# Fourier mixing with a SoLU layer on one core: the down products of a unit taken four steps behind its h instead of three

## The chip, the cores and the metric

The kernel runs on one core of a Trainium2 chip. The metric is the device time of one execution in microseconds, as the median of three runs. Before the change it is 1402.14 us (1400.0, 1402.14 and 1403.6).

## The reference, cut to what matters

Two blocks follow one another. The first is the real part of a Fourier transform over the sequence and the features of x, 8 x 3136 x 256. The second treats each of the 25088 rows of that result as a token.

```python
X = np.fft.fft(np.fft.fft(x, axis=1), axis=2).real      # 8 x 3136 x 256
h = X.reshape(25088, 256) @ w_in                        # 256 -> 1024
e = np.exp(h - h.max(-1, keepdims=True))
solu = h * e / (e.sum(-1, keepdims=True) + 1e-9)
ln = (solu - mean(solu)) / sqrt(var(solu) + 1e-6) * g_ln
out = ln @ w_out                                        # 1024 -> 256
```

## The kernel before

**Tiling.** The batch is worked on in four pairs of sequences. The sequence transform of 3136 = 49 x 64 points is split in two: a first transform over the 49 (transform1, L151), whose result goes through DRAM to be turned (the tile zd, written by SP at L156; the tile g, read by POOL at L163), and a second one over the 64 (transform2, L174 and L176). The feature transform is folded into the matrix Wi, so the product with Wi gives h at once. By symmetry only 25 of the 49 residues k1 are transformed; each gives two groups of 128 rows of the output, of signs 0 and 1 (k1 = 0 gives one).

A **unit** is one pair p and one k1. There are 100 units, and the main loop runs one step per unit. The steps in which a unit is worked on are these:

- `up` (L200): 8 matmuls of 128 x 512 on PE give the even and the odd part of h in PSUM, in the tiles ps_h.
- `even` (L206) and `join` (L214, L219) on DVE put the parts together into h for each sign, with its maximum. `expo` (L225) on ACT takes the exponential into u.
- `product` (L233) on DVE makes u = h * u, `square` (L242) on ACT and a few small POOL instructions (`stats`) give the variance and so the factor rs of each row.
- `turn_blocks` (L269): DVE transposes u in blocks of 32 x 32 into the tile v. `move_blocks` (L278): 16 DMAs on SP bring the blocks of two units to their places in the tile uT. Two following units share a batch, and a batch has one tile v and one tile uT; of each there are two buffers. A batch is moved once its second unit is through, at the end of every odd step. In the last two steps each unit is moved alone.
- `down` (L284): for each sign 8 products of 128 x 128 by 128 x 256 with Wo (16 matmuls in the trace) into a PSUM tile ps_o. `scale` (L289) on ACT multiplies by rs, and one step later `store` writes the rows, sign 0 with SP (L300) and sign 1 with an indirect DMA on POOL (L296).

**The order.** It is written out by hand: `tc.manual_schedule()` keeps each engine's instructions in the order of the program, and only waits on data and buffers move them. In a step i, PE runs: up of unit i, transform2 of unit i+1, one piece of transform1 for the next pair (or POOL turns a piece of g), then the down products of an older unit, i - lag. DVE runs even, join, product and the transposes of unit i, then the fold of the next pair's input (L111 to L113), if it is due. SP runs the store of unit i - lag - 1, then a write of zd, then the moves of the batch, then loads of x.

The first transform of the next pair is worked on in steps k1 = 4 to 19 of the first three pairs, 48 steps in all; its turn in the steps 20 to 24.

The lines that matter around the change:

```python
small = ctx.enter_context(tc.tile_pool(name="small", bufs=6))
...
lag = 3
for i in range(len(units) + lag):
    old = units[i - lag] if i >= lag else None
    if i > lag:
        store(units[i - lag - 1])
...
    if old:
        ps_o = [down(old, s) for s in old.signs]
```

The pool small holds the per-row statistics of a unit (rs among them), in as many buffers for each name as bufs says.

Of the kernel before, what the change touches and what calls it, by code (L numbers as in the profile page):

```python
# [33 lines left out]
def kernel(  # L34
# [33 lines left out]
    zpool = ctx.enter_context(tc.tile_pool(name="zpool", bufs=2))  # L68
    gpool = ctx.enter_context(tc.tile_pool(name="gpool", bufs=6))
    qpool = ctx.enter_context(tc.tile_pool(name="qpool", bufs=3))  # L70
    small = ctx.enter_context(tc.tile_pool(name="small", bufs=6))
    dram = ctx.enter_context(tc.tile_pool(name="dram", bufs=2, space=bass.MemoryType.DRAM))
    ps_h = ctx.enter_context(tc.tile_pool(name="ps_h", bufs=1, space=PSUM))
    ps_m = ctx.enter_context(tc.tile_pool(name="ps_m", bufs=4, space=PSUM))
# [91 lines left out]
    def transform2(pr, k1):  # L166

        i, k = divmod(k1, KG)  # L170
        g = pr.g[i]
        ps = ps_m.tile([P, KD * P + 1], FP32, tag="m", name="ps2")
        for h in range(KD):
            nc.tensor.matmul(ps[:, h * P : (h + 1) * P], g[:, k, h * P : (h + 1) * P], T[:, k1, :],  # L174
                             start=(h == 0), stop=True, skip_group_check=True)
        nc.tensor.matmul(ps[:, KD * P :], T[:, k1, :], g[:, k, P : P + 1],  # L176
                         start=False, stop=True, skip_group_check=True)
        return ps

    def take2(ps):  # L180
        q = qpool.tile([P, KD * P + 1], FP32, tag="q", name="q")
        nc.scalar.copy(q, ps)  # L182
        return q
# [11 lines left out]
    def up(t, c):  # L195

        ps = ps_h.tile([P, FF], FP32, tag=f"h{c}", name=f"ps_h{c}")
        for half in range(2):
            fs = slice(half * HW, (half + 1) * HW)
            nc.tensor.matmul(ps[:, fs], t.q[:, c * P : (c + 1) * P], Wi[:, c, fs], start=True, stop=True)  # L200
        return ps

    def even(t, ps):

        t.ev = fpool.tile([P, FF], FP32, tag="ev", name="ev", bufs=1)
        nc.vector.scalar_tensor_tensor(out=t.ev, in0=w_mid, scalar=t.q[:, KD * P :], in1=ps,  # L206
                                       op0=ALU.mult, op1=ALU.add)

    def join(t, ps):

        t.nmax = small.tile([P, 2], FP32, tag="nmax", name="nmax")
        for s in t.signs:
            t.h[s] = fpool.tile([P, FF], FP32, tag="h", name="h", bufs=2)
            nc.vector.tensor_tensor_reduce(out=t.h[s], in0=t.ev, in1=ps, scale=1.0, scalar=-3.0e38,  # L214
                                           op0=ALU.subtract if s else ALU.add, op1=ALU.max,
                                           accum_out=t.nmax[:, s : s + 1])
        n = len(t.signs)
        t.neg = small.tile([P, 2], FP32, tag="neg", name="neg")
        nc.vector.tensor_scalar(out=t.neg[:, 0:n], in0=t.nmax[:, 0:n], scalar1=-1.0, scalar2=None, op0=ALU.mult)  # L219

    def expo(t):
        t.esum = small.tile([P, 2], FP32, tag="esum", name="esum")
        for s in t.signs:
            t.u[s] = fpool.tile([P, FF], FP32, tag="u", name="u", bufs=2)
            nc.scalar.activation(out=t.u[s], in_=t.h[s], func=ACT.Exp, bias=t.neg[:, s : s + 1],  # L225
                                 accum_out=t.esum[:, s : s + 1])

    def product(t, s):

        if s == 0:  # L230
            t.usum = small.tile([P, 2], FP32, tag="usum", name="usum")
            t.nmean = small.tile([P, 2], FP32, tag="nmean", name="nmean")
        nc.vector.scalar_tensor_tensor(out=t.u[s], in0=t.h[s], scalar=1.0, in1=t.u[s], op0=ALU.mult,  # L233
                                       op1=ALU.mult, accum_out=t.usum[:, s : s + 1])
        nc.gpsimd.tensor_scalar(out=t.nmean[:, s : s + 1], in0=t.usum[:, s : s + 1], scalar1=-1.0 / FF,  # L235
                                scalar2=None, op0=ALU.mult)

    def square(t, s):

        if s == 0:  # L240
            t.ssq = small.tile([P, 2], FP32, tag="ssq", name="ssq")
        nc.scalar.activation(out=t.h[s], in_=t.u[s], func=ACT.Square, bias=t.nmean[:, s : s + 1],  # L242
                             accum_out=t.ssq[:, s : s + 1])
# [36 lines left out]
    def down(t, s):  # L280
        uT = t.batch.uT[:, t.w].rearrange("p c i (n s) -> p c (i n) s", s=2)
        ps = ps_m.tile([P, D], FP32, tag="m", name="ps_o")
        for c in range(KF):
            nc.tensor.matmul(ps, uT[:, c, :, s], Wo[:, c, :], start=(c == 0), stop=(c == KF - 1))  # L284
        return ps
# [5 lines left out]
    def store(t):  # L291

        for s in t.signs:
            if s:
                i = NP * NC + t.p * (NK - 1) + t.k1 - 1
                dma = nc.gpsimd.indirect_dma_start(  # L296
                    out=out, out_offset=bass.IndirectOffsetOnAxis(ap=idx[:, i : i + 1], axis=0),
                    in_=t.ot[s], in_offset=None)
            else:
                dma = nc.sync.dma_start(out=out_k[t.p, t.k1], in_=t.ot[s])  # L300

            tc.declare_no_dep(dma.ins, group=f"out{1 - s}", reason="other rows of the output")
            tc.add_to_no_dep_group(f"out{s}", dma.ins)
# [92 lines left out]
    def ahead(pr, step):  # L396

        c, r = divmod(step - 2, 2)
        if step == 0:
            load(pr, 0)  # L400
            load(pr, 1)
        elif 0 <= c < NC:
            if r == 0:
                add_mirror(pr, c)
            else:
                fold(pr, c)
                if c + 2 < NC:
                    load(pr, c + 2)

    def ahead_pe(pr, step):  # L410

        if 0 <= step - 4 < NH // 2:
            transform1(pr, step - 4)
        elif step - 4 >= NH // 2:
            turn(pr, step - 4 - NH // 2)

    with tc.manual_schedule():
        pairs = [Pair(p) for p in range(NP)]
        nc.sync.dma_start(out=idx, in_=mirror)
        nc.scalar.dma_start(out=F, in_=f_tab)  # L420
        ahead(pairs[0], 0)
        nc.vector.memset(ones, 1.0)
        nc.vector.memset(neg_half, -0.5)
        nc.vector.memset(T, 0.0)
        with tc.tile_pool(name="prep", bufs=1) as prep:
            prepare = load_weights(prep)
            for step in range(1, NK):
                ahead(pairs[0], step)
                ahead_pe(pairs[0], step)
            prepare()  # L430
        fpool = ctx.enter_context(tc.tile_pool(name="fpool", bufs=2))

        units = [Unit(p, k1) for p in range(NP) for k1 in range(NK)]
        units[0].q = take2(transform2(pairs[0], 0))
        lag = 3
        for i in range(len(units) + lag):
            cur = units[i] if i < len(units) else None
            nxt = units[i + 1] if i + 1 < len(units) else None
            old = units[i - lag] if i >= lag else None
            ahd = pairs[cur.p + 1] if cur and cur.p + 1 < NP else None  # L440
            last = i >= len(units) - 2
            if i > lag:
                store(units[i - lag - 1])
            if cur:
                if i % 2 == 0:
                    batch = Batch()
                cur.batch, cur.w = batch, i % 2
                even(cur, up(cur, 0))
                odd = up(cur, 1)
            if nxt:  # L450
                nxt.q = take2(transform2(pairs[nxt.p], nxt.k1))
            if cur:
                join(cur, odd)
                expo(cur)
            if ahd:
                ahead_pe(ahd, cur.k1)
            if old:
                ps_o = [down(old, s) for s in old.signs]
            if cur:
                for s in cur.signs:  # L460
                    product(cur, s)
                for s in cur.signs:
                    square(cur, s)
                    turn_blocks(cur, s)
            if old:
                scale(old, 0, ps_o[0])
            if cur:
                if last:
                    move_blocks(batch, slice(cur.w, cur.w + 1))
                elif cur.w:  # L470
                    move_blocks(batch, slice(0, 2))
                stats(cur)
            if ahd:
                ahead(ahd, cur.k1)
            if old and 1 in old.signs:
                scale(old, 1, ps_o[1])
        store(units[-1])
# [76 lines left out]
```

## Time and profile before

| | |
|---|---|
| median of three runs | 1402.14 us (1400.0 to 1403.6) |
| profiled execution | 1403.22 us, its span 1401.4 us |
| mean granted clock of TensorE | 0.935 of full speed |
| busy share | PE 87%, DVE 69%, ACT 44%, POOL 40% |
| main loop | first up matmuls at 139.3 us, last at 1358.7 us |

The span is the time from the first to the last instruction; what lies outside it is 1.8 us. Until about 139 us the kernel loads the weights and prepares them, and does the first pair's transform. The main loop of 100 steps takes the rest. Engines are named as in the profile: PE is TensorE, DVE VectorE, ACT ScalarE, POOL GpSimd, and SPq is the queue of SyncE, which issues DMAs.

### The profile page before, as it was taken

The numbers are of one execution on the slowest core, as the hardware profiler recorded it, in microseconds if no ns is written. First come the engines' busy times: TensorE is split into PE (matmuls) and PEld (weight loads), VectorE is DVE, ScalarE is ACT, GpSimd is POOL, SyncE is SP. The second block draws the span as 40 slices with busy tenths as digits, with TensorE's granted clock in tenths as the row PEclk, the third lists the DMA queues.
The fourth block names the chain that finished last, engine by engine and source line by source line (L and its number), as shares of the span: only waits on it lengthen the run. The fifth ranks groups of instructions, "written<-read, shape, count | busy, mean of one in ns | idle before, by whom it ended". The sixth has DMA issues, their size and how long they took to land.

```text
span 1401.4 us, 15865 instructions
## 1 busy us (share of the span) xinstructions
PE 1219.9 (87%) x4864; PEld 919.1 (66%) x4864; DVE 960.7 (69%) x1481; ACT 614.0 (44%) x1149; POOL 555.8 (40%) x972
## 2 busy tenths in 40 slices
PE   1642599999998999999988999999988899998988
PEld 1311277777766667777766677777776676776667
DVE  2498877777765767777757667777765766676671
ACT  1100445545544545555544445455543544454452
POOL 3430344544354345454344335444353333332331
PEclk9566899999999989999999999999999999999998
DMA  9550469787798777877697597896888557565664
GB/s 244 185 128 0 83 120 172 146 163 136 142 165 150 132 156 136 163 159 139 130 180 141 101 167 143 149 162 129 148 157 151 90 89 134 94 107 105 110 115 92
DMA packets 464628, 189.53 MB, mean 135 GB/s; under 512 B 433206, under 2 KB 446782, under 8 KB 464288
## 3 DMA queue, kind: packets, MB, share of 16 engines
q1 hardware_dynamic: 444752, 144.45, 59.4%
q0 software_dynamic: 13824, 38.55, 10.3%
q10 hardware_dynamic: 5968, 5.52, 1.7%
q8 instruction: 40, 0.66, 0.2%
q14 instruction: 44, 0.36, 0.1%
HBM read 44.78 MB, written 38.80 MB: 60 GB/s over the span
## 4 chain that ended last, share of the span: by engine, by line
PE 64%; SPq 14%; DMA 9%; DVE 9%; issue 2%; ACT 1%; POOL 1%; POOLq 0%; DVEq 0%; ACTq 0%
PE ps_o L284 42%; PE ps_h L200 17%; SPq L278 13%; DMA out_dram<-ot 3%; DMA uT<-v 3%; DMA xa<-in_x_dram 2%; PE ps L151 2%; PE ps L174 2%; DVE ex L316 2%; DVE h L214 1%; DMA xb<-in_x_dram,idx 1%; DVE u L233 1%; ACT u L225 1%; POOL xa L120 1%; DVE v L269 1%
## 5 line engine op out<-in xcount | busy, mean ns | idle before, releaser
L284 PE MATMUL ps_o<-Wo,uT 128*128 128x256 f32 x3136 | 730.3, 393 | 75.3 <-DMA out_dram<-ot 44.1
L284 PEld LDWEIGHTS ps_o<-Wo,uT 128*128 128x128 f32 x3136 | 631.9, 203 | 153.1 <-issue 80.1
L200 PE MATMUL ps_h<-Wi,q 128*128 128x512 f32 x800 | 361.8, 595 | 8.8 <-DVE ev L206 7.3
L233 DVE SCALAR_TENSOR_TENSOR u<-h,u 128x1024 f32<-128x1024 f32 x196 | 232.5, 1223 | 139.5 <-ACT u L225 139.5
L235 POOL TENSOR_SCALAR nmean<-usum 128x1 f32<-128x1 f32 x196 | 128.6, 656 | 489.3 <-DVE u L233 489.0
L225 ACT ACTIVATE u<-h,neg 128x1024 f32<-128x1024 f32 x196 | 223.6, 1141 | 193.2 <-DVE neg L219 191.4
L242 ACT ACTIVATE h<-u,nmean 128x1024 f32<-128x1024 f32 x196 | 223.8, 1143 | 122.8 <-POOL nmean L235 122.8
L214 DVE CUSTOM_DVE_ANT_0 h<-ev,ps_h 128x1024 f32<-128x1024 f32 x196 | 231.7, 1219 | 50.3 <-PE ps_h L200 44.0
L200 PEld LDWEIGHTS ps_h<-Wi,q 128*128 128x128 f32 x800 | 152.2, 191 | 158.1 <-issue 146.5
L206 DVE SCALAR_TENSOR_TENSOR ev<-w_mid,q,ps_h 128x1024 f32<-128x1024 f32 x100 | 127.8, 1278 | 164.1 <-PE ps_h L200 158.9
L269 DVE STREAM_TRANSPOSE v<-u 128x1024 f32<-128x1024 f32 x200 | 238.8, 1236 | 0.1
L182 ACT COPY q<-ps 128x257 f32<-128x257 f32 x100 | 37.4, 374 | 250.4 <-PE ps L176 195.0
L296 POOL DMA_INDIRECT out_dram<-ot,idx x96 | 103.0, 1073 | 92.4 <-ACT ot L289 70.2
L289 ACT ACTIVATE ot<-ps_o,rs 128x256 f32<-128x256 f32 x196 | 82.9, 459 | 92.1 <-PE ps_o L284 89.1
L151 PE MATMUL ps<-y,F 98*100 98x258 f32 (+3 forms) x288 | 82.2, 427 | 44.9 <-DVE y L113 44.2
L254 POOL TENSOR_SCALAR v<-ssq 128x2 f32<-128x2 f32 (+1 forms) x100 | 26.5, 265 | 169.8 <-ACT h L242 169.8
L174 PEld LDWEIGHTS ps<-T,g 128*128 128x128 f32 x400 | 60.4, 191 | 47.4 <-issue 47.4
L151 PEld LDWEIGHTS ps<-y,F 98*100 98x100 f32 x288 | 48.7, 193 | 59.4 <-DVE y L113 25.6
L120 POOL TENSOR_TENSOR xa<-xa,xb 98x1020 f32<-98x1020 f32 (+1 forms) x32 | 72.7, 2272 | 28.6 <-DMA xa<-in_x_dram 19.9
L257 POOL TENSOR_TENSOR rs<-v,neg_half 128x2 f32<-128x2 f32 (+1 forms) x100 | 72.1, 721 | 7.8
L174 PE MATMUL ps<-T,g 128*128 128x128 f32 x400 | 60.7, 274 | 0.0
L163 POOL DMA_DIRECT2D g<-zd x80 | 47.9, 608 | 18.7 <-DMA zd<-z 11.3
(53 smaller groups left out, 492.9 us busy)
## 6 DMA issues: line engine op xcount, KB each, us to landing
uT<-v SPq DMA_DIRECT2D x784, 128.0 KB
zd<-z SPq DMA_DIRECT2D x32, 400.0 KB
g<-zd POOLq DMA_DIRECT2D x80, 160.0 KB, 5.1
out_dram<-ot SPq DMA_DIRECT2D x100, 128.0 KB
xa<-in_x_dram SPq DMA_DIRECT2D x32, 392.0 KB
raw_in_moe_w_in_dram<-in_moe_w_in_dram ACTq DMA_DIRECT2D x1, 2048.0 KB
raw_in_moe_w_out_dram<-in_moe_w_out_dram ACTq DMA_DIRECT2D x1, 2048.0 KB
uT<-v SPq DMA_DIRECT2D x32, 64.0 KB
```

The costliest lines, as they stand in the source:

```text
L151: nc.tensor.matmul(o[..., cs], F[:, 2 * t + h, :], i[..., cs], start=first, stop=True, skip_group_check=True)
L174: nc.tensor.matmul(ps[:, h * P : (h + 1) * P], g[:, k, h * P : (h + 1) * P], T[:, k1, :], start=(h == 0), stop=True, skip_group_check=True)
L200: nc.tensor.matmul(ps[:, fs], t.q[:, c * P : (c + 1) * P], Wi[:, c, fs], start=True, stop=True)
L206: nc.vector.scalar_tensor_tensor(out=t.ev, in0=w_mid, scalar=t.q[:, KD * P :], in1=ps, op0=ALU.mult, op1=ALU.add)
L214: nc.vector.tensor_tensor_reduce(out=t.h[s], in0=t.ev, in1=ps, scale=1.0, scalar=-3.0e38, op0=ALU.subtract if s else ALU.add, op1=ALU.max, ...
L225: nc.scalar.activation(out=t.u[s], in_=t.h[s], func=ACT.Exp, bias=t.neg[:, s : s + 1], accum_out=t.esum[:, s : s + 1])
L233: nc.vector.scalar_tensor_tensor(out=t.u[s], in0=t.h[s], scalar=1.0, in1=t.u[s], op0=ALU.mult, op1=ALU.mult, accum_out=t.usum[:, s : s + 1])
L235: nc.gpsimd.tensor_scalar(out=t.nmean[:, s : s + 1], in0=t.usum[:, s : s + 1], scalar1=-1.0 / FF, scalar2=None, op0=ALU.mult)
L242: nc.scalar.activation(out=t.h[s], in_=t.u[s], func=ACT.Square, bias=t.nmean[:, s : s + 1], accum_out=t.ssq[:, s : s + 1])
L269: nc.vector.transpose(out=t.batch.v[:, t.w, :, o], in_=t.u[s])
L278: nc.sync.dma_start(out=uT[b, i], in_=v[a, q])
L284: nc.tensor.matmul(ps, uT[:, c, :, s], Wo[:, c, :], start=(c == 0), stop=(c == KF - 1))
```

## The change

The distance between a unit's h and its down products, `lag`, goes from 3 to 4. The scale, and the store one step behind it, go with the down products. The loop so runs one more step at its end, and its first four steps instead of three have no down products. The small statistics have seven buffers instead of six.

```diff
-    small = ctx.enter_context(tc.tile_pool(name="small", bufs=6))
+    small = ctx.enter_context(tc.tile_pool(name="small", bufs=7))
...
-        lag = 3
+        lag = 4
         for i in range(len(units) + lag):
```

## Rows read from the trace of the kernel before

**Rows 1.** The page's first part: busy us of each engine (share of the span).

```profile
PE 1219.9 (87%) x4864; PEld 919.1 (66%) x4864; DVE 960.7 (69%) x1481; ACT 614.0 (44%) x1149; POOL 555.8 (40%) x972
```

**Rows 2.** Waits of PE from 193 us on: us in total, times, longest us.

```profile
PE ps_o L284 <- DMA out_dram<-ot: 44.1, 13, 6.4
PE ps_o L284 <- DMA uT<-v: 16.3, 6, 6.2
PE ps L151 <- DVE y L113: 4.0, 2, 2.0
PE ps_o L284 <- issue: 3.2, 4, 2.6
PE ps_o L284 <- DMA xa<-in_x_dram: 2.9, 1, 2.9
```

**Rows 3.** Timeline of PE, a step without T1: start us, us, operation [idle before].

```profile
738.99 3.60 PE L200 MATMUL ps_h<-Wi,q 128*128 128x512 f32 x8
...
743.01 7.16 PE L284 MATMUL ps_o<-Wo,uT 128*128 128x256 f32 x32
750.01 3.60 PE L200 MATMUL ps_h<-Wi,q 128*128 128x512 f32 x8
```

**Rows 4.** Timeline of PE, a step with T1.

```profile
601.59 3.60 PE L200 MATMUL ps_h<-Wi,q 128*128 128x512 f32 x8
...
606.53 7.07 PE L284 MATMUL ps_o<-Wo,uT 128*128 128x256 f32 x32
613.44 3.60 PE L200 MATMUL ps_h<-Wi,q 128*128 128x512 f32 x8
```

**Rows 5.** Timeline of DVE at the end of the step of rows 3.

```profile
749.03 2.37 DVE L269 STREAM_TRANSPOSE v<-u 128x1024 f32<-128x1024 f32 x2
751.93 1.28 DVE L206 SCALAR_TENSOR_TENSOR ev<-w_mid,q,ps_h 128x1024 f32<-128x1024 f32 x1 [0.52 <-PE ps_h L200]
```

**Rows 6.** Timeline of SP's queue: moves and stores at five places.

```profile
698.34 14.56 SPq L278 DMA_DIRECT2D uT<-v  x16
713.00 1.21 SPq L300 DMA_DIRECT2D out_dram<-ot  x2
...
751.47 13.28 SPq L278 DMA_DIRECT2D uT<-v  x16
...
1300.48 13.18 SPq L278 DMA_DIRECT2D uT<-v  x16
...
1375.29 10.44 SPq L278 DMA_DIRECT2D uT<-v  x16
```

**Rows 7.** Timeline of PE: down products that waited, with their idle time before.

```profile
718.54 9.60 PE L284 MATMUL ps_o<-Wo,uT 128*128 128x256 f32 x32 [6.41 <-DMA out_dram<-ot]
...
1316.99 8.84 PE L284 MATMUL ps_o<-Wo,uT 128*128 128x256 f32 x32 [2.83 <-DMA out_dram<-ot]
...
1365.91 30.90 PE L284 MATMUL ps_o<-Wo,uT 128*128 128x256 f32 x128 [3.60 <-DMA out_dram<-ot]
```

**Rows 8.** Groups of PE from 193 us on, L284: busy us, mean ns | idle.

```profile
L284 PE MATMUL ps_o<-Wo,uT 128*128 128x256 f32 x3091 | 717.5, 392 | 66.6 <-DMA out_dram<-ot 44.1 <-DMA uT<-v 16.3 <-issue 3.2
```

**Rows 9.** The same group in 578 to 662 us, where PE hardly waited.

```profile
L284 PE MATMUL ps_o<-Wo,uT 128*128 128x256 f32 x225 | 50.0, 380 | 0.1
```

**Rows 10.** Windows: us, busy PE, PEld, DVE, ACT, POOL, clock, DMA share, GB/s.

```profile
578.00:662.00 84.00, 83.91 (x353) 64.04 (x352) 63.50 (x94) 44.05 (x85) 40.37 (x66) 1.00 0.80 151
...
1002.00:1072.00 70.00, 61.42 (x247) 46.32 (x246) 48.37 (x68) 32.89 (x62) 34.91 (x68) 0.97 0.90 160
```

**Rows 11.** Timeline of PE at the start: the first and the third down products.

```profile
175.13 6.49 PE L284 MATMUL ps_o<-Wo,uT 128*128 128x256 f32 x16 [8.73 <-DMA uT<-v]
...
198.26 7.07 PE L284 MATMUL ps_o<-Wo,uT 128*128 128x256 f32 x32
```

**Rows 12.** Timeline of DVE: the end of the first fold in the loop.

```profile
180.30 0.16 DVE L113 COPY y<-xa 98x8 f32<-98x8 f32 x1
```

**Rows 13.** Waits of SP's queue from 193 us on: us, times, longest.

```profile
SPq L278 <- PE ps_o L284: 1.4, 3, 0.6
```

## The prediction

> **What bounds the kernel now.** I read the page's engine shares first: PE is busy 87% of the span, DVE 69%, ACT 44% [rows 1]. So PE is the engine whose idle time counts. Then its waits from 193 us on, where every step has its down products: L284 (the down matmuls) waits 24 times (13 + 6 + 4 + 1), 66.5 us in all, and nothing else holds PE but two waits of L151, 4.0 us [rows 2]. The up matmuls never wait there.
>
> Next, what a step takes when nothing waits. Call S(i) the start of the up matmuls of step i, and T1 the first transform, which is in 48 of the 100 steps. Without T1 a step lasts 750.01 - 738.99 = 11.02 us, and its down products start 743.01 - 738.99 = 4.02 us after S and take 7.00 us [rows 3]. With T1 it lasts 613.44 - 601.59 = 11.85 us, the down products start 4.94 us after S and take 6.91 us [rows 4].
>
> Then who is late for the down products: the 16 moves of a batch (v to uT) on SP. The transposes that fill v end at 749.03 + 2.37 = 751.40, 1.4 us into the next step [rows 5], and the moves start at 751.47 [rows 6], 1.46 us after S = 750.01. From the first issue to PE's start I find 20.2 us at the longest (698.34 to 718.54) and 16.5 us at the shortest (1300.48 to 1316.99) [rows 6, 7]. These are upper bounds of the landing, since PE was waiting.
>
> Now the arithmetic of a lag of three. The batch of units 2b and 2b+1 is moved from S(2b+2) + 1.46, and its first use is the down of unit 2b in step 2b+3. Between the two lie 11.02 + 4.02 - 1.46 = 13.6 us without T1, 11.85 + 4.94 - 1.46 = 15.3 us with it. Needed are 16.5 to 20.2. So it is late by 1.2 to 6.6 us. After such a wait the next batch is in time (DVE doesn't wait with PE, so its moves have gained what PE lost), and the one behind it is late again: one wait in four steps, and 24 in some 96 steps is what the rows count.
>
> **The change, part by part.**
>
> *The waits.* With a lag of four the first use is the down of step 2b+4: 13.6 + 11.02 = 24.6 us after the first issue without T1, 27.2 with it. Against 16.5 to 20.2 that leaves 4.4 us at the worst. So all waits of L284 go: -66.6 us [rows 8]. What is late next? DVE: its even part waited 0.52 us for PE in an undisturbed step [rows 5], so DVE has a little under PE's pace and PE stays the bound.
>
> *The clock.* After a wait of several us the next down pair is slow: 9.60 us after the wait of 6.41 us, against 7.0 [rows 3, 7]. Over everything: 3091 down matmuls took 717.5 us [rows 8]; in an undisturbed stretch with the granted clock at 1.00 (the 2.4 GHz level), 225 took 50.0 us, 0.2222 us each [rows 9, 10]. 3091 x 0.2222 = 686.9, so 30.6 us were lost to slower down products behind waits. They go with the waits: -30.6 us.
>
> *The start.* One step more runs without down products. Before, PE stood idle 8.73 us for the first batch, did unit 0 (one product) in 6.5 us from 175.13, and started its down products of step 5 at 198.26, which is S(5) + 4.94, so S(5) = 193.3 with units 0 and 1 done [rows 11]. After, PE does step 4 in that gap, held only by the fold for T1, which ends at 180.30 + 0.16 = 180.46 [rows 12]. T1 takes 4.94 - 4.02 = 0.92 us more; then unit 0 at the slow 6.5 us of the row (PE has idled as before), so S(5) = 187.9 with unit 0 alone done. Unit 1 costs 6.9 more: 194.8 against 193.3, +1.5 us. Were unit 0 at full pace (3.5 us), it would be -1.5.
>
> *The end.* One pair more is left behind the last up matmuls. Before, four pairs ran without a gap from 1365.91, after a wait of 3.60 [rows 7]. After, five run from 1362.3 on that scale, so unit 99 comes up at 1362.3 + 4 x 7.0 = 1390.3. Its moves are all issued at 1375.29 + 10.44 = 1385.7 [rows 6]; the smallest tail behind a last issue in the rows is 1316.99 - (1300.48 + 13.18) = 3.3 us [rows 6, 7], so they land near 1389. That is covered by about 1 us: 0, and 1.0 us if the tail is as long as 718.54 - (698.34 + 14.56) = 5.6 us. The extra pair itself is no extra work: it is the one that left the start.
>
> *SP and POOL.* Each step issues the same moves, stores, loads and turns in the same order; a store belongs to a unit one older. Per two steps SP issues 13.3 us of moves and 1.2 us of stores [rows 6] out of 22, so its order costs 0. The seventh small buffer holds the statistics one step longer: no time. The one new tie is uT: the moves of batch b+2 must wait until the down of unit 2b+1 has read the buffer, which is now in step 2b+5, the step that ends with these moves. That down ends at S(2b+6), the transposes at S(2b+6) + 1.4 [rows 3, 5]: covered by 1.4 us, and if PE is later than that the moves have 4.4 us more. Cost 0, bound 0 to 3 us.
>
> *The sum* is made on the profiled execution, span 1401.4: -66.6 - 30.6 + 1.5 + 0 = 1305.7, plus the 1.8 us that its run had outside the span: 1307.5. That run, 1403.2, is 1.1 us (0.08%) over the median, which I leave.
>
> The row of the DMA engines is a share of 0.80 in an undisturbed stretch with T1, but 0.90 between 1002 and 1072, where pairs change and g is turned [rows 10]. The Trainium skill (DMA: Bandwidth & Descriptors, Specifications) wants at least 512 bytes in a transfer for line rate, and the pieces that the moves carry are 64 elements of v, 256 bytes. By that rule the engines would be short before PE is, and the time would be that of the first rival.
>
> **The rivals.**
>
> 1. *DMA at the change of pairs.* In 1002 to 1072 the engines moved 0.90 x 70 = 63.0 us of work beside 61.4 us of PE [rows 10]. At PE's pace they fall behind by a few us in each of the three changes, and landing comes later than 24.6 us. For: the longest landings (20.2) are there. Against: the spare is 4.4 us or more, and a few us of arrears in 60 fit into it. If two waits survive in each change at half of the dearest (6.41 idle + 2.6 slow clock, so 4.5), 6 x 4.5 = 27: **1334.5**. At full price 1361.5.
> 2. *The store is what PE waits for.* The trace names out_dram<-ot for 44.1 us of the wait [rows 2]. If it is that, not uT, this part stays with its share of the clock: 44.1 + 30.6 x 44.1/66.6 = 64.4: **1372**. Against: down reads no output, and the store is issued at 713.00, just behind the last move [rows 6], so it lands with it.
> 3. *It does nothing,* because a total rate (SP's issues or the DMA engines) sets the pace and the waits come back a step later: **1403**. Against: 84 us without a wait at a share of 0.80 [rows 10].
> 4. *Slower: uT is held too long.* Two uT buffers now serve batches that live a step longer. It decides if a buffer is released more than 4.4 us behind the transposes. Were it held until the down of the following step, moves and PE would be tied: 16.5 to 20.2 us of landing against 11.0 + 4.0 = 15.0, so 1.5 to 5.2 us of wait in each of 49 batches, 3.4 in the middle, each with 30.6/24 = 1.3 us of slow clock: 49 x 4.7 = 230: **1537.5**. For: SP waits for ps_o at all (1.4 us, 3 times) [rows 13]. Against: those waits are under 0.6 us, and the last reader is in the moves' own step. The Trainium skill (Perfetto Trace Analysis, Optimization Strategy) says of a gap that repeats on the engine that should be saturated that buffers may be too few. By that rule the deeper lag takes from what is scarce and this rival holds; the 13.6 us against 16.5 speak for a late transfer.
>
> **How the numbers follow.** Forecast 0.78, rival 1 0.12, rival 2 0.03, rival 3 0.03, rival 4 0.04. A change of 0.3% (4 us) is about what a measurement of this kernel can tell from none. Faster: 0.78 + 0.12 + 0.03 = 0.93; same 0.03; slower 0.04. Range: down from 1307.5 by the 4.0 us of L151, 3.0 of the start, 1.1 of the median and 2 of the runs' spread: 1297. Up by the bounds of the end (1) and of uT (3), then on over rival 1 at its half price (1334.5) and a little beyond: 1340.
>
> **What would show it.** Right: L284 waits under 5 us from 193 us on, steps of 11.0 and 11.9 us throughout, a granted clock near 1.00 in the loop, and a mean of 0.222 us per down matmul. The moves should still start 1.4 to 1.5 us into a step. Wrong: L284 still waiting where g is turned (rival 1), SP waiting for ps_o for whole us (rival 4), or PE now held by DVE at L200.

## The result and the profile after

The changed kernel takes 1300.59 us (median of four runs, 1298.94 to 1302.77) against 1401.07 us in the same comparison: a ratio of 0.9284, 95% interval 0.9261 to 0.9307. Forecast were 1307.5 us, with a range of 1297 to 1340. The profiled execution took 1302.77 us, its span 1301.0 us.

First the page's engine line of the changed kernel, which answers to [rows 1], and then one row of its windows over nearly the whole loop (columns as in [rows 10]).

```profile
PE 1184.9 (91%) x4864; PEld 899.4 (69%) x4864; DVE 959.6 (74%) x1481; ACT 610.2 (47%) x1149; POOL 554.1 (43%) x972
```

```profile
193.00:1250.00 1057.00, 1057.00 (x4454) 813.55 (x4453) 815.17 (x1187) 558.22 (x1056) 483.16 (x866) 1.00 0.68 151
```

PE is busy in 1057.00 of 1057.00 us, with the granted clock at 1.00 (2.4 GHz) throughout. DVE's work has not changed (960 us), only its share. The waits of PE from 193 us on and the group of L284, which answer to [rows 2, 8], say the same:

```profile
PE ps_o L284 <- DMA uT<-v: 2.7, 1, 2.7
```

```profile
L284 PE MATMUL ps_o<-Wo,uT 128*128 128x256 f32 x3120 | 695.2, 381 | 2.7 <-DMA uT<-v 2.7
```

24 waits have become one, and that one lies in the tail. A down matmul takes 695.2/3120 = 0.2228 us on average, where 717.5/3091 = 0.2321 stood before and 0.2222 in an undisturbed stretch. PE's timeline in the middle of the loop, as in [rows 3, 4], where a pair of sequences has just changed:

```profile
739.95 3.60 PE L200 MATMUL ps_h<-Wi,q 128*128 128x512 f32 x8
...
743.97 7.16 PE L284 MATMUL ps_o<-Wo,uT 128*128 128x256 f32 x32
750.96 3.60 PE L200 MATMUL ps_h<-Wi,q 128*128 128x512 f32 x8
...
754.98 1.09 PE L151 MATMUL ps<-y,F 98*100 98x258 f32 x4
755.90 3.62 PE L284 MATMUL ps_o<-Wo,uT 128*128 128x256 f32 x16
759.36 3.60 PE L200 MATMUL ps_h<-Wi,q 128*128 128x512 f32 x8
```

The step without T1 lasts 11.01 us. The next has the first T1 of a pair and the short down of a unit with one sign. With a lag of three that short down came one step earlier, ahead of the first T1, so PE got there before the fold and waited: the 4.0 us of L151 in [rows 2], which are gone.

**Where the 100.4 us of the span came from.** For this I need three points of the kernel before that are not among the rows ahead: the starts of steps 0, 5 and 99 (the last).

```profile
139.26 3.70 PE L200 MATMUL ps_h<-Wi,q 128*128 128x512 f32 x8 [0.47 <-ACT q L182]
...
193.31 3.60 PE L200 MATMUL ps_h<-Wi,q 128*128 128x512 f32 x8
```

```profile
1358.71 3.60 PE L200 MATMUL ps_h<-Wi,q 128*128 128x512 f32 x8
```

The same points of the changed kernel, from PE's timeline at the start (steps 0, 4 and 5, with what stands between the last two) and at the end:

```profile
140.47 3.70 PE L200 MATMUL ps_h<-Wi,q 128*128 128x512 f32 x8 [0.46 <-ACT q L182]
...
171.77 5.23 PE L200 MATMUL ps_h<-Wi,q 128*128 128x512 f32 x8 [4.30 <-DVE ev L206]
...
181.74 2.02 PE L151 MATMUL ps<-y,F 98*100 98x258 f32 x4 [4.18 <-DVE y L113]
183.56 4.41 PE L284 MATMUL ps_o<-Wo,uT 128*128 128x256 f32 x16
187.80 3.60 PE L200 MATMUL ps_h<-Wi,q 128*128 128x512 f32 x8
```

```profile
1253.60 3.60 PE L200 MATMUL ps_h<-Wi,q 128*128 128x512 f32 x8
1257.03 27.79 PE L284 MATMUL ps_o<-Wo,uT 128*128 128x256 f32 x128
1287.48 8.84 PE L284 MATMUL ps_o<-Wo,uT 128*128 128x256 f32 x32 [2.66 <-DMA uT<-v]
```

| stretch | before | after | difference |
|---|---|---|---|
| to the first up matmuls | 139.26 | 140.47 | +1.2 |
| S(0) to S(5), where S(5) was 193.31 | 54.05 | 47.33 | -6.7 |
| S(5) to S(99), as many products on both sides | 1165.40 | 1065.80 | -99.6 |
| S(99) to the end of the span | 42.69 | 47.40 | +4.7 |

The first row is outside the loop. The second and the fourth belong together: a down pair (the products of one unit's two signs, 7.0 us) has left the start and stands at the end. The gain is all in the loop. For the third row, the windows of both kernels (columns as in [rows 10]) and the group of L284 in them, before and after in turn:

```profile
193.31:1358.71 1165.40, 1098.43 (x4489) 837.74 (x4488) 821.58 (x1194) 565.58 (x1065) 487.95 (x873) 0.97 0.75 138
```

```profile
187.80:1253.60 1065.80, 1065.80 (x4490) 819.91 (x4488) 823.47 (x1199) 564.10 (x1069) 487.51 (x876) 1.00 0.69 151
```

```profile
L284 PE MATMUL ps_o<-Wo,uT 128*128 128x256 f32 x2961 | 686.2, 391 | 63.0 <-DMA out_dram<-ot 40.5 <-DMA uT<-v 16.3 <-issue 3.2
```

```profile
L284 PE MATMUL ps_o<-Wo,uT 128*128 128x256 f32 x2961 | 658.9, 381 | 0.0
```

PE's idle time, 1165.40 - 1098.43 = 67.0 us, is gone, and its busy time has fallen by 32.6 us.

The tail holds the one wait that is left. SP's queue there, and what it waited for from 193 us on (us, times, longest), which answers to [rows 13]:

```profile
1244.04 13.18 SPq L278 DMA_DIRECT2D uT<-v  x16
1257.32 0.75 SPq L300 DMA_DIRECT2D out_dram<-ot  x1
1264.13 10.40 SPq L278 DMA_DIRECT2D uT<-v  x16
1274.63 0.54 SPq L300 DMA_DIRECT2D out_dram<-ot  x1
1275.28 10.40 SPq L278 DMA_DIRECT2D uT<-v  x16
```

```profile
SPq L278 <- PE ps_o L284: 7.8, 3, 6.0
```

The moves of unit 98 could have started at 1258.1, behind the store. They start at 1264.13, when PE has read unit 95 out of the same uT buffer: 1257.03 + 7.0 = 1264.0. All later moves shift with them, and unit 99 arrives 2.7 us late, with a slow down pair behind it (8.84 us).

### The profile page after: what moved, and what is told of

Same layout as the page of the kernel before. It is cut to its first block, busy times and chain, and to the rows that moved or that the text cites. A ratio compares the mean times of both kernels' runs of the same rounds, so it can differ in the third digit from the quotient of the medians.

```text
span 1301.0 us, 15863 instructions
## 1 busy us (share of the span) xinstructions
PE 1184.9 (91%) x4864; PEld 899.4 (69%) x4864; DVE 959.6 (74%) x1481; ACT 610.2 (47%) x1149; POOL 554.1 (43%) x972
## 3 DMA queue, kind: packets, MB, share of 16 engines
q1 hardware_dynamic: 444752, 144.45, 51.1%
## 4 chain that ended last, share of the span: by engine, by line
PE 86%; DVE 8%; DMA 3%; issue 1%; POOL 1%; ACT 0%; POOLq 0%; DVEq 0%; ACTq 0%
PE ps_o L284 52%; PE ps_h L200 25%; PE ps L151 4%; PE ps L174 3%; DMA xa<-in_x_dram 2%; DVE ex L316 2%; DMA xb<-in_x_dram,idx 1%; PE ps L176 1%; POOL xa L120 1%; DVE u L233 1%; DVE h L214 1%; DVE v L269 1%; DVE rest L344 0%; DVE rest L346 0%; DVE unit L334 0%
## 5 line engine op out<-in xcount | busy, mean ns | idle before, releaser
L284 PE MATMUL ps_o<-Wo,uT 128*128 128x256 f32 x3136 | 699.6, 381 | 2.7 <-DMA uT<-v 2.7
L284 PEld LDWEIGHTS ps_o<-Wo,uT 128*128 128x128 f32 x3136 | 613.3, 197 | 65.2 <-issue 3.5
L200 PE MATMUL ps_h<-Wi,q 128*128 128x512 f32 x800 | 363.3, 597 | 13.1 <-DVE ev L206 11.6
L151 PE MATMUL ps<-y,F 98*100 98x258 f32 (+3 forms) x288 | 81.2, 422 | 47.0 <-DVE y L113 47.0
L151 PEld LDWEIGHTS ps<-y,F 98*100 98x100 f32 x288 | 48.4, 192 | 61.0 <-DVE y L113 26.9
```

Source lines behind the costliest of these rows:

```text
L151: nc.tensor.matmul(o[..., cs], F[:, 2 * t + h, :], i[..., cs], start=first, stop=True, skip_group_check=True)
```

## Experiments

My theory: the moves of a batch land 16.5 to 20.2 us after their first issue (so in all 24 waits of the kernel before), a lag of three gives them 13.6 to 15.3 us, a lag of four 24.6 or more, and nothing else matters. Each time stands against the kernel before as it ran on the same chip (medians of 1399.9 to 1401.2 us).

**The lag alone.**

```diff
-    small = ctx.enter_context(tc.tile_pool(name="small", bufs=7))
+    small = ctx.enter_context(tc.tile_pool(name="small", bufs=6))
```

> Lag of four, but the small statistics keep six buffers. Theory (the transfer from v to uT has 24.6 us instead of 13.6 until it is needed, and nothing else matters): the time of the changed kernel, 1300.6 us within 3, since a factor rs is read at most four steps after it is written. Rival (the seventh buffer frees POOL or ACT of a wait and is part of the gain): 1310 us or more.

Measured: 1300.78 us, ratio 0.9284 (0.9262 to 0.9306), and the one wait of 2.7 us. The seventh small buffer has no part in the gain.

**Is it the store that PE waits for?** The lag of three, with no stores by SP.

```diff
             else:
-                dma = nc.sync.dma_start(out=out_k[t.p, t.k1], in_=t.ot[s])
+                continue
```

> Lag of three; the rows of sign 0 are not stored (half of the output is left out), so SP issues no stores in the loop. Theory (PE waits for the last move, the store only lands beside it): L284 still waits 55 to 67 us from 193 us on, and the time is 1385 to 1401 us. Rival (PE waits for the store that the trace names): the 44 us named for out_dram<-ot go, L284 waits 15 to 25 us, and the time is about 1340 us.

Measured in one run: 1401.33 us. Its longest waits of PE from 193 us on:

```profile
PE ps_o L284 <- DMA uT<-v: 33.7, 11, 6.1
PE ps_o L284 <- issue: 25.7, 13, 4.0
PE ps L151 <- DVE y L113: 4.0, 2, 2.0
```

L284 waits 62.5 us in all (two small entries, 3.2 us, make up the rest). Where the store was named before, mostly uT or nothing is named now. The name in [rows 2] was that of the transfer that ended last, not of the one that was needed. Rival 2 falls.

**A lag of three with the time of a lag of four.** If each unit is moved at the end of its own step, both units of a batch have 24.6 us with the old lag.

```diff
-                if last:
-                    move_blocks(batch, slice(cur.w, cur.w + 1))
-                elif cur.w:
-                    move_blocks(batch, slice(0, 2))
+                move_blocks(batch, slice(cur.w, cur.w + 1))
```

> Lag of three, but each unit is moved at the end of its own step, in 16 moves of half the size, instead of two units together. Both units then have two steps and a bit from the first issue to the use, 24.6 us without T1 and 27.2 with it, as a lag of four gives a batch. Theory (time from move to use is all): L284 waits under 15 us, 1300 to 1320 us; SP issues 2 x 10.4 us of moves and 1.2 us of stores in two steps of 22.0, so a little may come back there. Rival (the lag itself matters, by the order of the work on PE, or by when uT and the small buffers are freed): 1390 us or more.

Measured: 1367.82 us, ratio 0.9774 (0.9749 to 0.9800); L284 waits 41.7 us. A miss of both. SP's queue shows why:

```profile
1155.27 10.40 SPq L278 DMA_DIRECT2D uT<-v  x16
1165.77 0.54 SPq L300 DMA_DIRECT2D out_dram<-ot  x1
1166.42 10.75 SPq L278 DMA_DIRECT2D uT<-v  x16
1177.27 0.54 SPq L300 DMA_DIRECT2D out_dram<-ot  x1
```

From 1155.27 to 1166.42 are 11.15 us for 16 moves and a store, with gaps of 0.1 us, where PE needs 11.02: the issues of twice as many moves fill the queue, and it sets the pace. In steps with T1, where a load and a write of zd come between, the queue needs more: 13.1 us (the moves start at 564.49 and again at 577.56) where PE needs 11.85. So the run says little on the lag. The next one takes the load off SP: POOL issues 4 of the 16 moves.

```diff
+                e = nc.gpsimd if q == 3 else nc.sync
-                nc.sync.dma_start(out=uT[b, i], in_=v[a, q])
+                e.dma_start(out=uT[b, i], in_=v[a, q])
```

(Each unit is moved at the end of its own step, as in the run above, and `stats` goes ahead of the moves, so that POOL has it first.)

> Lag of three, each unit moved at the end of its own step, and 4 of its 16 moves issued by POOL instead of SP. In the run that left all 16 to SP its queue was never idle (10.4 to 12 us of moves and 0.6 to 1.2 of other issues in a step of 11.0 or 11.85). Now SP issues about 8 us of moves in a step. Theory (time from first issue to use, 24.6 us, is all, as long as SP isn't full): L284 waits under 10 us, 1298 to 1312 us. Rival (a lag of three is too short whatever SP does, by the order on PE): 1340 us or more. Rival (POOL, with 2.4 us more of issues in a step, holds the squares and the stores): 1320 us or more with ACT and POOL in the waits.

Measured: 1309.38 us, ratio 0.9351 (0.9321 to 0.9381), with a lag of **three**. The group of L284 from 193 us on (the edit moves it to L285):

```profile
L285 PE MATMUL ps_o<-Wo,uT 128*128 128x256 f32 x3097 | 691.5, 382 | 0.0
```

L285 has no wait at all, with the old lag. What matters is the time from issue to use, not the lag. (Two queues issue here, so the landing may be shorter as well; the run doesn't separate the two.) What the run takes more than the changed kernel, 9 us, comes from where T1 sets in: PE's timeline in the second pair shows

```profile
476.95 2.02 PE L151 MATMUL ps<-y,F 98*100 98x258 f32 x4 [4.09 <-DVE y L113]
478.77 9.23 PE L285 MATMUL ps_o<-Wo,uT 128*128 128x256 f32 x32
```

This is the wait for the fold that a lag of four avoids, with a slow down pair behind it. There are two such waits, 7.8 us in all; the tail, where nothing waits, gives a part back.

**Three uT buffers.**

```diff
-    gpool = ctx.enter_context(tc.tile_pool(name="gpool", bufs=6))
+    gpool = ctx.enter_context(tc.tile_pool(name="gpool", bufs=5))
...
-            self.uT = fpool.tile([P, 2, KF, 4, 64], FP32, tag="uT", name="uT", bufs=2)
+            self.uT = fpool.tile([P, 2, KF, 4, 64], FP32, tag="uT", name="uT", bufs=3)
```

> Lag of four with three uT buffers (and five g buffers instead of six, to make room). Theory: in the loop nothing changes (49 x 0), but in the last step the moves of unit 98 no longer wait 6 us for the down of unit 95, so unit 99 is there when PE comes to it: the wait of 2.7 us and 1.8 us of slow clock go, 1296 us. Rival (two uT buffers hold the loop too, the moves start late): a gain of 10 us or more. Rival (the end is set by SP's 2 x 10.4 us of issues, not by the buffer): no gain, 1300.6.

Measured: 1295.94 us, ratio 0.9246 (0.9227 to 0.9265), so about 4.7 us less than the changed kernel. PE has no wait from 193 us on, and the tail runs through; here PE's and SP's last rows:

```profile
1255.86 34.70 PE L284 MATMUL ps_o<-Wo,uT 128*128 128x256 f32 x160
```

```profile
1256.15 0.74 SPq L300 DMA_DIRECT2D out_dram<-ot  x1
1257.00 11.27 SPq L278 DMA_DIRECT2D uT<-v  x16
```

The moves of unit 98 now start 0.1 us behind the store. In the loop two buffers are enough, so rival 4 holds only in the last step, at a price of 4.7 us.

**One step more, and the start.** The lag of five with three uT buffers, five g buffers and eight small ones:

```diff
-        lag = 4
+        lag = 5
```

> Lag of five, three uT buffers, eight small ones. Theory (from a lag of four on PE itself is the bound, steps of 11.02 and 11.85 us): nothing is left to gain in the loop; 1296 us within 3, as a lag of four with three uT buffers, since the pair that leaves the start comes back at the end. Rival (some waits under 0.1 us or the clock still leave something in a lag of four): 1290 us or less.

Measured: 1306.76 us, ratio 0.9337 (0.9306 to 0.9367), a miss: 10.8 us more than a lag of four with three uT buffers. Its PE at the start:

```profile
179.30 1.11 PE L151 MATMUL ps<-y,F 98*100 98x258 f32 x4 [4.04 <-DVE y L113]
180.57 5.30 PE L200 MATMUL ps_h<-Wi,q 128*128 128x512 f32 x8 [0.16 <-DVE ev L206]
...
200.59 2.00 PE L151 MATMUL ps<-y,F 98*100 98x258 f32 x4 [5.02 <-DVE y L113]
```

The pair that leaves the start gives no time back, because DVE (the fold above all) sets the pace of the first steps and PE only waits longer for it. At the end the pair costs its full 7.0 us. In the loop the wait for the fold is back at the two later pairs, 7.7 - 5.0 = 2.7 us by PE's waits from 193 us on:

```profile
PE ps L151 <- DVE y L113: 7.7, 3, 5.0
```

The other attempt at the start moves the first T1 behind the first down product, on top of three uT buffers:

```diff
-            if ahd:
+            if ahd and i != lag:
                 ahead_pe(ahd, cur.k1)
             if old:
                 ps_o = [down(old, s) for s in old.signs]
+            if ahd and i == lag:
+                ahead_pe(ahd, cur.k1)
```

> Lag of four with three uT buffers, and in step 4 alone the first piece of transform1 goes behind the down product of unit 0 instead of ahead of it, so PE does the down product while it waits for the fold (4.2 us idle in the changed kernel). Theory (everything in between is bound by PE, so only the two ends can still give): 2.8 us less than with three uT buffers alone, 1293 us. Rival (DVE holds step 5 anyway): 1296 us.

Measured: 1297.47 us, ratio 0.9264 (0.9238 to 0.9290), no gain over 1295.94: the theory misses, and the rival holds. The same place of its PE:

```profile
180.93 1.11 PE L151 MATMUL ps<-y,F 98*100 98x258 f32 x4 [0.33 <-DVE y L113]
...
202.22 1.37 PE L151 MATMUL ps<-y,F 98*100 98x258 f32 x4 [3.05 <-DVE y L113]
```

The first wait shrinks from 4.2 to 0.3 us and comes back at the next fold. That second T1 starts 62.6 us after the first up matmuls in both runs (200.59 - 138.03 and 202.22 - 139.64), whatever PE does in between: DVE holds the start.

**The other edit alone, and where uT lies.** The profiles had shown something that I could not explain: the same 444752 packets of the SP queue took 63.7% of the span with six small buffers and 51.1% with seven. The lag of three with seven of them:

```diff
-    small = ctx.enter_context(tc.tile_pool(name="small", bufs=6))
+    small = ctx.enter_context(tc.tile_pool(name="small", bufs=7))
```

> Lag of three with seven small buffers, which moves v and uT by 320 bytes in memory; with a lag of four the DMA engines' time for the same 444752 packets of the SP queue was 63.7% of 1299.4 us with six buffers and 51.1% of 1301.0 with seven. Theory (16 issues of SP, 13.3 us, set most of the landing, and what the packets take only its tail): the share falls likewise, L284 waits 45 to 66 us, 1375 to 1401 us. Rival (the shorter packets bring the moves in early enough, and this is where the gain of the change is from): 1350 us or less.

Measured: 1405.37 us, ratio 1.0046 (1.0019 to 1.0072); L284 waits 66.1 us. The share fell to 47.9% of 1397.4 us, and no time was gained: the rival falls, though the time lies a little above the theory's range. Then v and uT were put at multiples of 512 bytes, with a lag of four (and three uT buffers) by the tile below, and with a lag of three and six small buffers by one of 8 elements:

```diff
+    pad = small.tile([P, 56], FP32, tag="pad", name="pad", bufs=1)
...
+        nc.vector.memset(pad, 0.0)
```

> Lag of four with three uT buffers, and an unused tile of 224 bytes that moves v and uT to multiples of 512 bytes (they lay 288 behind one with seven small buffers, 480 with six). Theory (where v and uT lie sets what a packet takes; PE is the bound): the share of the SP queue falls below the 51.4% of 1295.2 us, the time stays at 1296 us within 3. Rival (the share differs for another reason): 51 to 52% again. Rival (shorter packets still give time): 1290 us or less.

> Lag of three, six small buffers, and an unused tile of 32 bytes that moves v and uT to multiples of 512 bytes. Theory (16 issues of SP set the landing): the share of the SP queue falls from 59.4% to 48% or less, and yet L284 waits 50 us or more and the time is 1380 to 1405 us. Rival (the packets set the landing): 1360 us or less.

Measured: with a lag of four 1295.43 us, ratio 0.9243 (0.9193 to 0.9292), the time as expected and the share lower, at 43.5%. With a lag of **three** 1323.72 us, ratio 0.9449 (0.9398 to 0.9501): the theory as I had written it for this run is wrong, and the time lies where the rival had it. Its group of L284 (now L285), three batches of moves, and behind them one of the run with seven small buffers:

```profile
L285 PE MATMUL ps_o<-Wo,uT 128*128 128x256 f32 x3088 | 690.8, 382 | 16.8 <-DMA out_dram<-ot 9.1 <-issue 3.6 <-DMA uT<-v 2.8
```

```profile
1046.86 11.01 SPq L279 DMA_DIRECT2D uT<-v  x16
...
1245.80 11.04 SPq L279 DMA_DIRECT2D uT<-v  x16
...
1267.83 11.02 SPq L279 DMA_DIRECT2D uT<-v  x16
```

```profile
1247.66 13.13 SPq L278 DMA_DIRECT2D uT<-v  x16
```

The 16 issues take 11.0 us here instead of 13.2, though they are the same instructions, so the pace of SP's issues is not a fixed cost of the queue. What sets it is open: with seven small buffers the packets' share had fallen too, and the issues still took 13.1 us. The landing gets shorter: from the first issue to PE's start are 13.2 us in the loop's shortest case (1046.86 to 1060.04, a row shown at the end of this document), where 16.5 was the shortest before. That is about what a lag of three has, and 50 of the 66.6 us of waits go. So the size of the landing was a second handle on the same cause: more time for the moves, or faster moves.

## Why the prediction was right, and where it was off

*The bound and the arithmetic of the lag.* Right. PE waited for uT, one wait in four steps; with 24.6 us the waits are gone from the loop, and DVE does not take their place. The moves still start 1.5 us into a step: S is 1242.6 by the 11.0 us of a step before 1253.60, the moves start at 1244.04. The runs put the cause on the time between issue and use: the lag alone has the whole gain, leaving out SP's stores and a seventh small buffer change nothing, a lag of three whose units have 24.6 us has no wait for uT (that run changes the moves' size and queue too), and with faster moves most of the waits go at a lag of three.

*The size.* The span came out at 1301.0, with 1305.7 forecast. By the stretches: in the loop the sum had 66.6 - 3.6 = 63.0 us of waits (the last is the tail's) and 27.5 of the 30.6 us of slow clock (a tail of 30.90 us instead of the 27.79 of the changed kernel holds the rest), 90.5 together. Measured were 99.6. The waits of L284 were 63.0, as forecast, and its matmuls took 686.2 - 658.9 = 27.3 us less, nearly as forecast. Of the 9.1 us more, 4.0 are the waits of L151, which the prediction had only in the range. The others are busy time: 1.1 us of L151, and some 4 that stay open. No other line's matmuls changed by as much as 1 us, but matmuls that follow one another overlap, and a wait may break that; no run separates it. The total is nearer than its parts, partly by luck: the loop gained 9.1 us more than forecast, and the tail took 4.5 us more.

*The start.* Forecast were +1.5 us with a slow first product of 6.5; it took 4.4 (183.56), and T1 ahead of it 2.0 instead of 1.1. By the table, -6.7 + 6.9 for the pair = +0.2. That S(5) came at 187.80, with 187.9 forecast, is luck: the loop had begun 1.2 us later.

*The end.* Here a step failed: "That is covered by about 1 us". The prediction let the moves of unit 98 start as before, and weighed the tie of uT to the down products for the loop alone. In the last two steps the units are moved one by one, so a move there comes ahead of the down of unit 95 in time but needs its buffer. That cost 2.7 us of wait and 1.8 of slow clock; the three buffers gave 4.7 us back.

*The rivals.* The DMA engines at the change of pairs: nothing waits there. Its price rested on 0.90 x 70 = 63 us "of work", and this was a wrong reading: the share is not a fixed amount of work, as the table below shows. The Trainium skill (DMA: Bandwidth & Descriptors, Specifications) wants 512 bytes for line rate. The pieces of 256 bytes did not become the bound here, at 151 GB/s over the loop; what pieces of 512 would take no run shows. The store, and no effect at all, are ruled out by the runs. On the buffers, the Trainium skill's rule on repeating gaps (Perfetto Trace Analysis, Optimization Strategy) offers too few buffers as a cause. For uT this was not the cause in the loop: before, SP waited only 1.4 us for a buffer [rows 13], and with a lag of four two buffers leave PE no wait in the loop. A third buffer was not tried with a lag of three; the gap was a late transfer.

## What to carry to other kernels

When an engine that should be full waits for a transfer, write down the time from the transfer's first issue to its first use, and the time it needs, both from the timeline: if the first is shorter, the wait and its period follow, and here one more step of distance gave the whole of it back. Then look at the ends: a deeper pipeline moves work from the start to the tail, which is free only while the engine is the bound there, and a buffer that was long free in the loop may be held in the last step. A lag of four with a third uT buffer (1295.9 us) is better than both kernels; a lag of five (1306.8 us) is not.

## What was not expected of the hardware

The time that the DMA engines spend on the same 444752 packets of the SP queue depends on where v and uT lie. The page's row of that queue, in turn for the kernel before, the changed kernel, and a lag of four with uT at 512:

```profile
q1 hardware_dynamic: 444752, 144.45, 59.4%
```

```profile
q1 hardware_dynamic: 444752, 144.45, 51.1%
```

```profile
q1 hardware_dynamic: 444752, 144.45, 43.5%
```

| v and uT behind a multiple of 512 bytes by | share x span, lag of three | share x span, lag of four |
|---|---|---|
| 480 bytes | 832 us (before) | 828 us (the lag alone) |
| 288 bytes | 669 us (seven small buffers) | 665 us (the changed kernel) |
| 0 bytes | 562 us | 563 us |

The offsets are those of the programs' memory layout, which no trace shows; the buffers behind v and uT move along with them. The time goes with the offset and not with the lag. The lag of five, whose eight small buffers put v and uT 96 bytes behind, is out of this order: 53.1% of 1304.9 us, 693 us. Only the step to 0 made the landing shorter; from 480 to 288 a fifth of the engines' time went and no wait with it, and why is open. So in this kernel the share of busy DMA engines says neither how much room is left nor how soon a transfer lands.

The clock behind a wait is not told by the length of the wait alone. In the run with a lag of three and uT at 512, PE's timeline has these two:

```profile
1060.04 7.15 PE L285 MATMUL ps_o<-Wo,uT 128*128 128x256 f32 x32 [2.91 <-DMA out_dram<-ot]
...
1303.83 8.84 PE L285 MATMUL ps_o<-Wo,uT 128*128 128x256 f32 x32 [2.12 <-issue]
```

The longer wait was followed by a pair at full pace, the shorter one by a slow pair. The granted clock was 1.00 (2.4 GHz) from 1059 to 1068 us. Behind the shorter wait it was 0.50 (1.2 GHz) from 1306 to 1308 us and 0.99 again from 1308 to 1310.
